# One Trainium2 core, attention and two MoE layers: attention tiles of two heads of both batches, h in matmuls over 64 rows, and phase A in program order

## The chip, the cores and the metric

The kernel runs on one core of a Trainium2 chip. The metric is the device time of one execution in microseconds (us). Times below are in us unless they say ns. The engines are TensorE (PE; its weight loads are listed apart as PEld), VectorE (DVE), ScalarE (ACT), GpSimd (POOL) and SyncE (SP), which issues all DMAs of this kernel.

## What is computed

An attention with 32 memory slots per head, then two layers on its rows (8 batches of 8 heads, 576 positions, head size 64):

```python
a = phi - np.max(phi, axis=2, keepdims=True); a = np.exp(a)
a = a / (np.sum(a, axis=2, keepdims=True) + 1e-09)
k_m = np.einsum('bhsm,bhsd->bhmd', a, k)
v_m = np.einsum('bhsm,bhsd->bhmd', a, v)
scores = (1 / 8) * np.matmul(q, k_m.transpose(0, 1, 3, 2))   # then a softmax over the 32
x = np.matmul(attn, v_m)                                     # as 4608 rows of 512
h = np.maximum(np.maximum(x @ w1, x @ w2), x @ w3)           # 768 wide
x = h @ w_out
...
gate = 1.0 / (1.0 + np.exp(-(x @ w_gate)))                   # 1536 wide
out = (gate * (x @ w_val)) @ w_out2
```

q, k, v and phi are 32-bit; the weights arrive as 64-bit floats.

## The kernel before

**Numbers.** Each operand of a large matmul is split into a high and a low part (type fp32r), and each product is three matmuls (`PASSES`: low by high, high by low, high by high). The 64-bit weights are turned to 32 bits in `w_f32`: two ACT and three DVE instructions on a tile of 128x384 (tiles `raw`, `ca`, `cr`, lines 122 to 126).

**Phase A** computes the attention and the first layer for four pairs of batches (p = 0 to 3) and writes the result x2 to memory. Phase B, from line 667 on, is the second layer; it begins when phase A ends, and the change leaves its code alone.

**Attention tiles.** One tile n holds four heads of one batch: 4 x 32 memory slots are its 128 rows, so a pair of batches has four tiles. A tile runs through stages a0 to a5 (lines 174 to 274): softmax of phi over its positions, a transpose, k_m and v_m in `kvb` (line 206, matmuls that write 32 columns of the array each, four side by side), their transposes (`kt` and the split `vt`), the scores (line 243, 64 columns each, two side by side), and the softmax over 32 slots, which ends in `stg`; `a_split` makes the split tile `attn` (128 x 576) of it.

**G.** x itself is never formed. Since x = attn v_m, x @ w = attn (v_m @ w): `g_step` (line 334 on) makes G = v_m @ w for two heads and for a block j of 128 of the 768 columns of the three weights (384 columns). One result of 128 rows holds 64 rows of one batch and 64 of the other; they go to two tiles, so that each is copied out and split in two halves of 64 rows: two ACT copies (line 354) and two subtractions (line 73), on DVE, or for the first head pair in p = 0 on POOL.

**h.** `h_step(p, j, u)` makes h for a block j and a quarter u of the pair's rows: u is a batch b and a half of its 576 positions (288). For each of the three weights 6 matmuls over all 128 rows (two groups of four heads, three passes) fill one PSUM bank; ACT copies the first, DVE takes the maximum with the second and third, and the result is split into `h`.

**x2.** `x2_step` multiplies h by the first w_out: 18 matmuls for each of 4 blocks of 128 columns and 4 quarters.

**Order.** A pair has 40 steps s: 24 for h (6 blocks j by 4 quarters, with G for block j + 1 beside them in the first 20) and 16 for x2 (with G for the next pair's block 0 in the last four). The attention stages of the next pair, the weights' conversions (`w_step` for the first layer, `b_step` for the 48 tiles of phase B, in pairs 1 to 3 by the program) and the loads are laid beside the steps by position. The program order is only a wish: except for the first loads, the tile framework's scheduler may move each instruction on each engine, by its own timeline. PSUM has 8 banks of 128 x 512, shared by all of phase A (`bank`).

In the parts below, "h stretch" and "x2 stretch" are the parts of a pair from its first matmul of line 367 and of line 390 on.

Of the kernel before, what the change touches and what calls it, by code (L numbers as in the profile page):

```python
# [18 lines left out]
def attn_moe_kernel(  # L19
# [11 lines left out]
    nc = tc.nc  # L31
# [16 lines left out]
    vec, act, pool, pe, sync = nc.vector, nc.scalar, nc.gpsimd, nc.tensor, nc.sync  # L48

    queue = {"in order": True, "last weights": None}  # L50
# [6 lines left out]

    def later(fn, *a):

        with tc.issue_after(queue["last weights"].ins):  # L60
            fn(*a)
# [43 lines left out]
    def w_fetch(pl, src):  # L105
        if not is64:
            w = pl.tile([128, PC], F32, tag="wf", name="wf", bufs=3)
            queue["last weights"] = dma(w, src)
            return w
        raw = pl.tile([128, PC], I64, tag="raw", name="raw", bufs=3)  # L110
        queue["last weights"] = dma(raw, src)
        return raw
# [24 lines left out]
    def early(shape):  # L137

        t = low.tile([128, 2 * U], F32R, tag="h", name="early", bufs=4 * J)
        return f32(t[:, :shape[1]])  # L140

    def load_phi(n):
        st = A[n] = {"kv": [], "q": []}
        if n in (2, 3):
            st["phi"] = early([128, S])
        else:
            st["phi"] = att.tile([128, S], F32, tag="phi", name="phi", bufs=2)
        dma(st["phi"], phiT[n])

    def load_kv(n):  # L150
        for c in range(5):
            if n < 4:
                t = early([128, 512])
            else:
                t = att.tile([128, 512], F32, tag="kv", name="kv", bufs=7)
            if c < 4:
                dma(t, kvm[n, c])
            else:
                dma(t[:64], kvt[n])
            A[n]["kv"].append(t)  # L160

    def load_q(n, e):
        if (n, e) in ((0, 0), (0, 1)):
            t = early([128, S])
        else:
            t = att.tile([128, S], F32, tag="q", name="q", bufs=3)
        dma(t, qT[n, e])
# [6 lines left out]
    def a0(n):  # L174
        st = A[n]
        nm = att.tile([128, 1], F32, tag="nm", name="nm", bufs=4)
        vec.tensor_reduce(out=nm, in_=st["phi"], axis=AX.X, op=ALU.max, negate=True)
        ss = att.tile([128, 1], F32, tag="ss", name="ss", bufs=4)
        et = st["et"] = att.tile([128, S], F32, tag="et", name="et", bufs=2)
        act.activation(out=et, in_=st["phi"], func=AF.Exp, bias=nm, accum_out=ss)  # L180
        rs = st["rs"] = att.tile([128, 1], F32, tag="rs", name="rs", bufs=4)
        vec.tensor_scalar(out=rs, in0=ss, scalar1=EPS, scalar2=None, op0=ALU.add)
        vec.reciprocal(out=rs, in_=rs)
        rm = st["rm"] = att.tile([128, 2], F32, tag="rm", name="rm", bufs=4)
        vec.tensor_scalar(out=rm, in0=mask, scalar1=rs, scalar2=None, op0=ALU.mult)
        yield

    def a1(n):
        st = A[n]
# [4 lines left out]
        yield  # L194
        es = st["es"] = att.tile([128, 5, 128], F32, tag="es", name="es", bufs=2)
# [3 lines left out]
    def a2(n):  # L199
# [20 lines left out]
    def a3(n):  # L220
        st = A[n]
        b, g = divmod(n, 2)
        p = bank()
# [5 lines left out]
        if b % 2 == 0:  # L229
            VT[b // 2, g] = mid.tile([128, 2, 4, 64], F32R, tag="vt", name="vt", bufs=4)  # L230
        vt = VT[b // 2, g]
        src = p[:, 128:256].rearrange("p (h m) -> p h m", h=2)
        for h in range(2):
            x = 3 * h if b % 2 == 0 else 2 - h
            act.copy(vt[:, 0, x], src[:, h])
            sub(vec, vt[:, 1, x], src[:, h], f32(vt[:, 0, x]))

    def a4(n):
# [10 lines left out]
        yield  # L249
        s_t = st["s"] = att.tile([128, S // 32, 32], F32, tag="s", name="s", bufs=2)  # L250
# [6 lines left out]
        mx = att.tile([128, S // 32], F32, tag="mx", name="mx", bufs=2)  # L257
        vec.tensor_reduce(out=mx, in_=s_t, axis=AX.X, op=ALU.max)
        bc = [128, S // 32, 32]
        sub(pool, s_t, s_t, mx.unsqueeze(2).to_broadcast(bc))  # L260
        act.activation(out=s_t, in_=s_t, func=AF.Exp, scale=SC)

    def a5(n):
        st = A[n]
        s_t = st["s"]
        bc = [128, S // 32, 32]
# [4 lines left out]
        pool.tensor_tensor(out=s_t, in0=s_t, in1=sm.unsqueeze(2).to_broadcast(bc), op=ALU.mult)  # L271
        stg = st["stg"] = att.tile([128, S], F32, tag="stg", name="stg", bufs=4)
        vec.transpose(out=stg, in_=s_t.rearrange("p a m -> p (a m)"))
        yield
# [10 lines left out]
    stages = [a0, a1, a2, a3, a4, a5]  # L285
# [13 lines left out]
    def w_have():  # L299
        j, hp, p, w = wq.pop(0)  # L300
        if j < 0:
            w = w_f32(mid, w)
            r = slice(hp * PC, hp * PC + PC)
            w_split(w, wo1_t[:, 0, r], wo1_t[:, 1, r])
            return
        if p == 0:
            w = w_f32(mid, w)
            t = mid.tile([128, 2, PC], F32R, tag="wx", name="wx", bufs=6)
            w_split(w, t[:, 0], t[:, 1])
            dma(wxs[j, hp], f32(t))  # L310
            w = t
        WX[j, hp] = w
# [9 lines left out]
    def b_step():  # L322
        if not bq:
            return
        b_want()
        i, n, w = bq.pop(0)
        dma(wbf[i, :, n * PC:n * PC + PC], w_f32(mid, w))
# [4 lines left out]
    def g_step(p, j, hp):  # L332
        g, e = divmod(hp, 2)
        if e == 0:
            for b in range(2):
                G[b, j, g] = mid.tile([128, 2, 384], F32R, tag=f"g{b}", name=f"g{b}", bufs=3 + b)
        ps = bank()
        vt, w = VT[p, g], WX.pop((j, hp))
        for n, (x, y) in enumerate(PASSES):
            pe.matmul(  # L340
                ps[:, :384],
                lhsT=vt[:, x, 2 * e:2 * e + 2].rearrange("p a m -> p (a m)"),
# [4 lines left out]
        src, eng = ps, vec  # L347
        if p == 0 and hp == 0:
# [518 lines left out]
```

## Time and profile before

| | |
|---|---|
| time, median of 3 runs | 1394.29 (1390.80 to 1395.04) |
| the profiled execution's own time | 1393.47 |
| its span, from first to last instruction | 1391.6 |
| ACT busy | 567.8 (41%), 1204 instructions |
| POOL busy | 519.3 (37%), 454 instructions |
| 1728 matmuls of h (line 367) | 254.6 busy |
| 1152 matmuls of x2 (line 390) | 158.4 busy |
| 288 matmuls of G (line 340) | 71.9 busy |
| mean granted PE clock | 0.986 |

Busy time counts the stretches in which an engine has an instruction under way; matmuls overlap, so that the mean length of one (301 ns for h) is longer than the distance from one to the next. A row of the chain of waits says when a piece of work on the chain that ended last began, how long it took, and which engine, tile and line it was. In a group of instructions the columns are line, engine, operation, tiles, shape, count, then busy time and the mean length of one in ns, then the idle time ahead of them and who ended it.

### The profile page before, as it was taken

What the parts mean: (1) busy time and instruction counts of PE and PEld (TensorE: products, weight loads), DVE (VectorE), ACT (ScalarE), POOL (GpSimd) and SP (SyncE); (2) the same over time, 40 slices, a digit from 0 to 9 for tenths busy, and PEclk for the clock granted to TensorE, in tenths of its full rate; (3) what the DMA queues carried; (4) which work ended last, traced back from release to release, by engine and by line L of the source; (5) the groups of instructions that cost most, each with busy time, mean ns of one, the idle gap of its engine ahead of it and who ended that gap; (6) DMA issues with size and microseconds to landing.
All of it is one profiled execution on the core that took longest, in us unless ns stands there. A gap on an engine that the chain in (4) does not pass through costs nothing.

```text
span 1391.6 us, 22154 instructions
## 1 busy us (share of the span) xinstructions
PE 1335.2 (96%) x7864; PEld 1184.2 (85%) x7864; DVE 872.3 (63%) x1549; ACT 567.8 (41%) x1204; POOL 519.3 (37%) x454
## 2 busy tenths in 40 slices
PE   5688998999999999999999999999999999999998
PEld 3587887889999999788888888888888899999997
DVE  5999989988773575667755345454454544554454
ACT  5787556755653452453343321232222322143221
POOL 2776512241342127554486111371112711161111
PEclk9799999999999999999999999999999999999999
DMA  9589799879644424865557554465455666566661
GB/s 309 192 285 300 258 305 311 287 262 305 212 133 139 129 82 137 295 258 211 202 190 228 175 176 159 155 207 190 158 178 169 217 221 221 195 229 231 221 207 66
DMA packets 112269, 292.43 MB, mean 210 GB/s; under 512 B 12576, under 2 KB 28960, under 8 KB 112160
## 3 DMA queue, kind: packets, MB, share of 16 engines
q1 hardware_dynamic: 112160, 291.03, 62.4%
q8 instruction: 62, 1.02, 0.3%
q14 instruction: 47, 0.39, 0.1%
HBM read 224.92 MB, written 66.06 MB: 209 GB/s over the span
## 4 chain that ended last, share of the span: by engine, by line
PE 80%; DVE 9%; DMA 5%; issue 3%; ACT 1%; POOL 1%; SPq 0%; DVEq 0%; ACTq 0%
PE po L752 21%; PE px L685 16%; PE ps L367 11%; PE pz L685 11%; PE pv L685 10%; PE ps L390 6%; PE ps L340 2%; DVE ca L126 2%; DVE g L73 1%; DVE ca L124 1%; DMA raw<-wb_dram 1%; DVE ca L125 1%; PE ps L206 1%; PE ps L243 1%; DVE hm L378 1%
## 5 line engine op out<-in xcount | busy, mean ns | idle before, releaser
L752 PE MATMUL po<-wo,gg 128*128 128x512 f32 x1296 | 327.7, 392 | 1.0 <-POOL gg L73 1.0
L73 POOL TENSOR_TENSOR gg<-gf,gg 128x512 fp32r<-128x512 f32 (+1 forms) x120 | 143.6, 1197 | 471.1 <-ACT gg L718 430.2
L752 PEld LDWEIGHTS po<-wo,gg 128*128 128x128 f32 x1296 | 242.4, 188 | 49.5 <-POOL gg L73 1.3
L367 PE MATMUL ps<-attn,g 128*128 128x288 f32 x1728 | 254.6, 301 | 19.4 <-DVE g L73 12.4
L367 PEld LDWEIGHTS ps<-attn,g 128*128 128x128 f32 x1728 | 244.2, 193 | 26.9 <-issue 14.0
L685 PE MATMUL px<-xa,tb 128*128 128x512 f32 (+1 forms) x1080 | 244.0, 368 | 3.2 <-DVE x L70 3.2
L764 DVE TENSOR_TENSOR acc<-po,acc 128x512 f32<-128x512 f32 x180 | 124.3, 690 | 176.4 <-PE po L752 176.3
L685 PEld LDWEIGHTS px<-xa,tb 128*128 128x128 f32 x1080 | 198.1, 188 | 31.5 <-DVE x L70 3.6
L685 PE MATMUL pv<-xa,tb 128*128 128x512 f32 (+1 forms) x720 | 169.2, 367 | 0.0
L685 PE MATMUL pz<-xa,tb 128*128 128x512 f32 (+1 forms) x720 | 169.1, 367 | 0.0
L390 PE MATMUL ps<-h,wo 128*128 128x288 f32 x1152 | 158.4, 296 | 0.6 <-DVE hm L379 0.6
L390 PEld LDWEIGHTS ps<-h,wo 128*128 128x128 f32 x1152 | 154.8, 189 | 2.7 <-DVE ca L126 0.9
L73 POOL TENSOR_TENSOR h<-hm,h 128x288 fp32r<-128x288 f32 x96 | 84.1, 880 | 194.0 <-ACT h L68 98.0
L685 PEld LDWEIGHTS pz<-xa,tb 128*128 128x128 f32 x720 | 132.1, 188 | 18.6
L685 PEld LDWEIGHTS pv<-xa,tb 128*128 128x128 f32 x720 | 131.9, 188 | 17.7
L718 ACT CAST gg<-gf 128x512 fp32r<-128x512 f32 (+1 forms) x120 | 69.4, 578 | 178.2 <-DVE gf L714 131.6
L736 DVE TENSOR_TENSOR u<-pz,p 128x512 f32<-128x512 f32 (+1 forms) x120 | 76.2, 635 | 97.8 <-PE pz L685 92.9
L73 DVE TENSOR_TENSOR g<-ps,g 64x384 fp32r<-64x384 f32 x180 | 99.2, 552 | 27.9 <-ACT g L354 24.9
L708 ACT ACTIVATE sg<-sg 128x512 f32<-128x512 f32 (+1 forms) x90 | 53.1, 590 | 144.3 <-DVE sg L706 144.1
L354 ACT CAST g<-ps 64x384 fp32r<-64x384 f32 x192 | 90.4, 472 | 50.8 <-PE ps L340 26.9
L73 POOL TENSOR_TENSOR xa<-xf,xa 128x512 fp32r<-128x512 f32 (+1 forms) x64 | 78.7, 1251 | 18.9 <-ACT xa L131 18.8
L714 DVE TENSOR_TENSOR gf<-gf,sg 128x512 f32<-128x512 f32 (+1 forms) x90 | 71.5, 795 | 9.5 <-ACT sg L708 1.3
(92 smaller groups left out, 1401.5 us busy)
## 6 DMA issues: line engine op xcount, KB each, us to landing
tb<-tbs SPq DMA_DIRECT2D x168, 512.0 KB, 3.8
wx<-wxs SPq DMA_DIRECT2D x72, 384.0 KB, 4.4
wo<-wos SPq DMA_DIRECT2D x48, 512.0 KB, 5.0
tbs<-tb SPq DMA_DIRECT2D x42, 512.0 KB, 2.9
raw<-wb_dram SPq DMA_DIRECT2D x48, 384.0 KB, 5.3
kv<-kvm_dram SPq DMA_DIRECT2D x48, 256.0 KB, 5.2
raw<-wx_dram SPq DMA_DIRECT2D x24, 384.0 KB, 4.3
wxs<-wx SPq DMA_DIRECT2D x24, 384.0 KB, 4.7
```

The costliest lines, as they stand in the source:

```text
L73: eng.tensor_tensor(out=o, in0=a, in1=b, op=ALU.subtract)
L126: vec.scalar_tensor_tensor(out=ai, in0=hi, scalar=0x80000000, in1=ai, op0=ALU.bitwise_and, op1=ALU.bitwise_or)
L354: act.copy(t[r, 0], ps[r, :384])
L367: pe.matmul(ps[w][:, :U], lhsT=G[b, j, g][:, x, 128 * w:128 * w + 128], rhs=at[:, y, hf * U:hf * U + U], start=(n == 0), stop=(n == 5),)
L390: pe.matmul(ps[:, :U], lhsT=wo1_t[:, x, (d * J + j) * 128:(d * J + j) * 128 + 128], rhs=H[u, j][:, y], start=(n == 0), stop=(n == 3 * J - 1),)
L685: pe.matmul(ps[:, :half], lhsT=w[:, a, o:o + 128], rhs=x[:, k, c, :half], start=(first and n == 0), stop=(n == 5), skip_group_check=not first,
L708: act.activation(out=sg, in_=src, func=AF.Sigmoid)
L714: vec.tensor_tensor(out=gf, in0=gf, in1=sg, op=ALU.mult)
L718: act.copy(t[:, 0, :half], gf)
L736: vec.tensor_tensor(out=u, in0=ps[:, :half], in1=E["p1", v], op=ALU.add)
L752: pe.matmul(ps, lhsT=GG[sc, j, c, h][:, x, 128 * m:128 * m + 128], rhs=WO[sc, j, h][:, y], start=(n == 0), stop=(n == 5),)
L764: vec.tensor_tensor(out=t, in0=ps, in1=t, op=ALU.add)
```

## The change

**Tiles.** An attention tile n now holds two heads of both batches of the pair: rows 0 to 63 are batch 0, rows 64 to 127 batch 1 (`source` gives the place in memory, and each load becomes two, of 64 rows, or of half the columns; k and v come in two chunks at once). Then one result of `g_step` is one tile of G: one ACT copy and one DVE subtraction over 128 rows. `vt` is likewise copied and split whole.

**h.** `h_part` makes h for a block j and a half hf of the positions, for both batches, in two steps of 36 matmuls. Each takes 64 rows of G and of `attn`, and those of the two batches alternate, rows 0 to 63 and then 64 to 127, into two different banks. A block and half needs 4 tiles of attention, 3 weights and 3 passes: 36 pairs. ACT copies the first weight's two banks (`h_copy`), DVE takes the maxima (`h_max`), ACT and POOL split both batches at once (`h_keep`).

**Order.** From the first step on, until x2 of the last pair, every compute instruction and DMA keeps the program's order on its engine. A step issues on PE the attention stages, G, then h or x2; then the copies; the conversion; the maximum with the second weight; what follows (the third weight's maximum, x2's copy, h's split, stores) is put off to the next step. The six attention stages become ten, one per step, each tile eight steps after the last. Four conversions of first-layer weights move from ahead of the first step into it, and phase B's conversions stand where the program has them: 13 in pair 1, 13 in pair 2, 22 in the h stretch of pair 3.

On PE, in the h stretch of pair 2, before the change (L340 is G, L367 h, L243 the scores; the numbers tell tiles of G apart):

```order
L340 MATMUL ps<-wx,vt 128x384 x3
L367 MATMUL ps<-attn,g_4841 128x288 x9
L243 MATMUL ps<-q,kt 64x288 x4
L367 MATMUL ps<-attn,g_4962 128x288 x9
L340 MATMUL ps<-wx,vt 128x384 x3
```

The same place in the change (L61 is the wrapper that all engines now go through; wx,vt is G, attn,g is h, each h matmul over 64 rows):

```order
L61 MATMUL ps<-ident,kvb 128x128 x2
L61 MATMUL ps<-wx,vt 128x384 x3
L61 MATMUL ps<-attn,g 128x288 x36
L61 MATMUL ps<-q,kt 64x288 x4
L61 MATMUL ps<-wx,vt 128x384 x3
L61 MATMUL ps<-attn,g 128x288 x36
```

The attention stage now stands ahead of G and G ahead of h, and h is never interrupted; 18 matmuls of a step have become 36.

On DVE, late in phase A before the change (hm are the maxima for h, g the subtractions for G over 64 rows):

```order
L378 TENSOR_TENSOR hm<-ps,hf 128x288
L379 TENSOR_TENSOR hm<-ps,hm 128x288
L73 TENSOR_TENSOR g_5285<-ps,g_5285 64x384
L70 CAST h<-hm 128x288
L378 TENSOR_TENSOR hm<-ps,hf 128x288
L73 TENSOR_TENSOR g_5284<-ps,g_5284 64x384
L379 TENSOR_TENSOR hm<-ps,hm 128x288
```

And in the h stretch of pair 3 in the change (the three instructions on ca are one conversion):

```order
L61 TENSOR_TENSOR hm<-ps,hm 128x288 x4
L61 TENSOR_TENSOR g<-ps,g 128x384
L61 TENSOR_SCALAR ca<-ca 128x384
L61 ISA ca<-ca,cr 128x768
L61 SCALAR_TENSOR_TENSOR ca<-raw,ca 128x384
L61 TENSOR_TENSOR g<-ps,g 128x384
```

The cast is gone to ACT, two subtractions have become one, and a conversion of phase B's weights stands in each step between the subtraction for G and the maxima.

The diff's core:

```diff
+    class InOrder:
...
+                ins = fn(*a, **k)
+                if order["kept"]:
+                    tc.keep_in_program_order(ins)
+    def source(n, b):
+        p, hp = divmod(n, 4)
+        g, pr = divmod(hp, 2)
+        return 2 * (2 * p + b) + g, pr ^ b
...
     def g_step(p, j, hp):
...
-        for hf in range(2):
-            r = slice(64 * hf, 64 * hf + 64)
-            t = G[(hf + e) % 2, j, g]
-            act.copy(t[r, 0], ps[r, :384])
-            sub(eng, t[r, 1], src[r, :384], f32(t[r, 0]))
+        t = G[j, hp] = mid.tile([128, 2, 384], F32R, tag="g", name="g", bufs=8)
+        act.copy(t[:, 0], ps[:, :384])
+        sub(vec, t[:, 1], ps[:, :384], f32(t[:, 0]))
...
+    def h_part(p, j, hf, first):
+        if first:
+            HP[j, hf] = []
+        for w, hp in [(w, hp) for w in range(3) for hp in range(4)][slice(0, 6) if first else slice(6, 12)]:
+            if hp == 0:
+                HP[j, hf].append([bank() for _ in range(2)])
+            at = AT[4 * p + hp]
+            for n, (x, y) in enumerate(PASSES):
+                for b in range(2):
+                    r = slice(64 * b, 64 * b + 64)
+                    pe.matmul(
+                        HP[j, hf][w][b][:, :U],
+                        lhsT=G[j, hp][r, x, 128 * w:128 * w + 128],
+                        rhs=at[r, y, hf * U:hf * U + U],
+                        start=(hp == 0 and n == 0), stop=(hp == 3 and n == 2),
+                    )
+    def h_max(j, hf, w):
+        m = HM[j, hf]
+        for b in range(2):
+            vec.tensor_tensor(out=m[:, b], in0=HP[j, hf][w][b][:, :U], in1=m[:, b], op=ALU.max)
+    def h_keep(j, hf):
+        m = HM.pop((j, hf))
...
+        act.copy(t[:, 0], m)
+        sub(pool, t[:, 1], m, f32(t[:, 0]))
...
-        t = low.tile([128, U], F32, tag="x2", name="x2", bufs=3)
+        t = low.tile([128, U], F32, tag="x2", name="x2", bufs=2)
...
+    order["kept"] = queue["in order"] = True
...
         for s in range(NS + NX):
             if last and s == NS:
+                order["kept"] = queue["in order"] = False
...
+            take("first")
+            gens = [stages[k](n) for k, n in sorted(atts.get(s, ()), reverse=True)]
+            for x in gens:
+                next(x)
+            g = None
             if s < NS:
                 j, u = divmod(s, 4)
                 if j + 1 < J:
+                    g = g_step(p, j + 1, u)
+                    next(g)
+                h_part(p, j, u // 2, u % 2 == 0)
...
+            if s < NS and u % 2:
+                h_copy(j, u // 2)
+            take("splits")
+            if g:
+                next(g, 1)
+            for x in gens:
+                next(x, 1)
+            take("hold")
             for fn, a in side.get(s, ()):
                 fn(*a)
+            for fn, a in convs.get(s, ()):
+                fn(*a)
+            if s < NS and u % 2:
+                h_max(j, u // 2, 1)
+                later["first"].append(lambda j=j, hf=u // 2: h_max(j, hf, 2))
+                hold.append(lambda j=j, hf=u // 2: h_keep(j, hf))
...
+            take("stores")
```

More of the change, by code (lines that the diff above doesn't have):

```diff
@@ L107, in w_fetch @@
             w = pl.tile([128, PC], F32, tag="wf", name="wf", bufs=3)
[L108 removed]
+            dma(w, src)
             return w
         raw = pl.tile([128, PC], I64, tag="raw", name="raw", bufs=3)
[L111 removed]
+        dma(raw, src)
         return raw
@@ L135, in attn_moe_kernel, with early_tile, early @@
     A = {}
-    def early(shape):
-        t = low.tile([128, 2 * U], F32R, tag="h", name="early", bufs=4 * J)
-        return f32(t[:, :shape[1]])
+    halves = []
+    def early_tile():
+        return f32(low.tile([128, 4 * U], F32R, tag="h", name="early", bufs=2 * J))
+    def early(cols):
+        if not halves:
+            t = early_tile()
+            halves.extend((t[:, :2 * U], t[:, 2 * U:]))
+        return halves.pop(0)[:, :cols]
+    def source(n, b):
+        p, hp = divmod(n, 4)
+        g, pr = divmod(hp, 2)
+        return 2 * (2 * p + b) + g, pr ^ b
     def load_phi(n):
@@ L228, in a3, with a5 @@
         act.copy(kt, p[:, 0:128])
[L229 to L238, printed above, removed]
+        vt = VT[n] = mid.tile([128, 2, 128], F32R, tag="vt", name="vt", bufs=8)
+        act.copy(vt[:, 0], p[:, 128:256])
+    def a5(n):
         st = A[n]
@@ L332, in g_step @@
     def g_step(p, j, hp):
[L333 to L336, printed above, removed]
         ps = bank()
-        vt, w = VT[p, g], WX.pop((j, hp))
+        vt, w = VT[4 * p + hp], WX.pop((j, hp))
         for n, (x, y) in enumerate(PASSES):
@@ L574, in attn_moe_kernel, with take, at @@
         run(g_step(0, 0, hp))
-    for hp in range(4):
-        w_step()
     bplan = [(j + h * NJ, n) for j in range(NJ) for h in range(2) for n in range(4)]
-    def b_start():
-        while len(bq) < 2 and bplan:
-            b_want()
+    order["kept"] = queue["in order"] = True
+    due = {"first": [], "splits": [], "hold": [], "stores": []}
+    def take(what):
+        fns, due[what] = due[what], []
+        for fn in fns:
+            fn()
     for p in range(NP):
         last = p == NP - 1
-        side = {}
-        def at(pos, fn, *a):
-            side.setdefault(min(int(pos), NS + NX - 1), []).append((fn, a))
+        side, loads, convs = {}, {}, {}
+        def at(pos, fn, *a, where=None):
+            where = side if where is None else where
+            where.setdefault(min(int(pos), NS + NX - 1), []).append((fn, a))
         if last:
```

272 lines of the change are left out of this document (152 added, 120 removed).

## The prediction

> **What bounds the kernel now.** I read first the page's span and its busy rows in 40 slices, to see where TensorE is not the bound.
>
> ```profile
> span 1391.6 us, 22154 instructions
> PE   5688998999999999999999999999999999999998
> DVE  5999989988773575667755345454454544554454
> ```
>
> TensorE (PE) is full from about slice 9 on; before that, VectorE (DVE) is as full as PE. Phase A, which the change touches, is the first 16 slices. So I cut it at the first matmul of each h stretch (line 367) and of each x2 stretch (line 390) of the four pairs of batches, and asked for the busy time of each engine in each piece. Columns: stretch, its length, then PE, weight load, DVE, ACT, POOL busy with instruction counts, granted PE clock, DMA share, GB/s.
>
> ```profile
> 0.00:50.80 50.80, 26.91 (x235) 14.83 (x235) 34.89 (x78) 29.22 (x73) 22.20 (x24) 0.88 0.91 291
> 50.80:150.30 99.50, 86.56 (x605) 79.17 (x605) 97.57 (x186) 75.52 (x178) 66.53 (x61) 0.92 0.77 259
> 150.30:203.70 53.40, 49.48 (x409) 45.89 (x410) 45.58 (x98) 29.51 (x71) 16.54 (x14) 0.97 0.90 294
> 203.70:294.00 90.30, 83.75 (x660) 76.74 (x658) 86.43 (x189) 61.18 (x148) 29.33 (x29) 0.96 0.86 291
> 294.00:339.60 45.60, 44.39 (x357) 42.73 (x356) 36.92 (x81) 24.40 (x57) 10.08 (x8) 1.00 0.90 297
> 339.60:418.50 78.90, 78.90 (x661) 74.61 (x660) 60.03 (x135) 46.58 (x114) 27.18 (x30) 1.00 0.56 175
> 418.50:462.40 43.90, 43.90 (x355) 42.54 (x354) 13.43 (x28) 11.09 (x26) 8.14 (x8) 1.00 0.41 136
> 462.40:529.70 67.30, 67.30 (x490) 67.30 (x490) 45.33 (x93) 34.46 (x82) 18.56 (x23) 1.00 0.31 93
> 529.70:572.50 42.80, 39.64 (x296) 39.02 (x294) 26.30 (x30) 13.28 (x24) 32.57 (x22) 1.00 0.67 229
> ```
>
> Pairs 0 to 3 have an h stretch and an x2 stretch each. Pair 2 does the same matmuls as pair 1, and takes 78.9 + 43.9 = 122.8 where pair 1 takes 90.3 + 45.6 = 135.9 and pair 0 99.5 + 53.4 = 152.9. In pairs 0 and 1 DVE is busy 97.57 of 99.5 and 86.43 of 90.3: **there it is DVE that ends last, in pairs 2 and 3 it is PE.** Pair 3 has no attention beside it: 67.3 is the bare length of 432 h matmuls and 60 for G, and 78.9 - 67.3 = 11.6 is what three tiles of attention add in pair 2, 3.9 each. The prize of relieving DVE is at most 152.9 + 135.9 - 2 x 122.8 = 43 of 1391.6.
>
> What fills DVE is in the same stretches for the conversions alone (three DVE instructions each; columns DVE, ACT, POOL):
>
> ```profile
> 50.80:150.30 99.50, 50.49 (x69) 23.81 (x45) 24.51 (x22) 0.92 0.77 259
> 203.70:294.00 90.30, 35.68 (x60) 10.89 (x20) 0.00 (x0) 0.96 0.86 291
> 339.60:418.50 78.90, 2.94 (x6) 1.11 (x2) 0.00 (x0) 1.00 0.56 175
> ```
>
> A conversion costs DVE 50.49 / 23 = 2.2 in pair 0 (with POOL busy) and 35.68 / 20 = 1.78 in pair 1. All 48 of phase B's are over early in pair 2: the scheduler pulls them forward.
>
> **The change, part by part.**
>
> *G's copies and the casts.* In DVE's groups from 50 to 150:
>
> ```profile
> L73 DVE TENSOR_TENSOR g<-ps,g 64x384 fp32r<-64x384 f32 x33 | 18.1, 550 | 0.6
> L70 DVE CAST h<-hm 128x288 fp32r<-128x288 f32 x6 | 3.2, 533 | 0.0
> ```
>
> Two subtractions over 64 rows become one over 128, taken at the same 0.55, since each row still has 384 elements. Pair 0 gave 12 of its 48 halves to POOL, so DVE goes from 36 to 24: 12 x 0.55 = 6.6 less; the casts go to ACT: 3.2 less; by the end of pair 0's h stretch 28 conversions are needed where 30 had been made: 4.4 less. That is 14, so DVE alone could end the stretch near 136. In pairs 1 to 3, 24, 24 and 20 subtractions go (13, 13, 11 us).
>
> *Pair 0's start.* A step now takes all four tiles of attention at once (line 409), so the first needs the fourth tile; now that one comes while the third step waits:
>
> ```profile
> 64.94 0.76 DVE L273 STREAM_TRANSPOSE stg<-s 128x576 f32<-128x576 f32 x1
> 66.47 1.81 PE L367 MATMUL ps<-attn,g 128*128 128x288 f32 x6 [1.20 <-ACT attn L281]
> ```
>
> In the new order DVE has one conversion, four half subtractions' worth, four maxima and a cast less ahead of that transpose, 2.2 + 2.2 + 1.8 + 1.1 = 7.3, so it comes near 58 and the first step passes its ninth pair near 60. From there PE's own length is 67.3, less 1.2 for the half step done, plus 2.2 tiles of attention, 8.5, plus the mode changes below, 6.8: end near 141.5. PE and DVE are then nearly equal; I allow 4 for their waiting on each other: 145.5, not 150.3. The x2 stretch becomes PE's: 43.9 with one tile of attention in it, and 1.75 tiles here, so 46.8. Pair 0 ends at 192 where it ended at 203.7: **-11.5.**
>
> *Pairs 1 and 2.* 13 conversions each, one in three steps: DVE falls in pair 1 to 86.4 - 35.7 - 13 - 3 + 8 x 1.78 = 49. Pair 1 comes to pair 2's length: **-13**; pair 2 gains nothing.
>
> *The h matmuls.* 1728 matmuls over 128 rows become 1728 pairs over 64 rows. Whether a pair goes side by side is not in the trace for rows; for columns it is (chain of waits, start, length, what):
>
> ```profile
> 418.17 0.44 PE ps L192 x4
> 418.60 0.11 PE ps L193
> 418.71 4.79 PE ps L390 x36
> 423.50 1.36 PE ps L206 x40
> 424.87 2.58 PE ps L390 x18
> 427.44 0.22 PE ps L225 x2
> 427.66 2.37 PE ps L390 x18
> ```
>
> A matmul over the full array with 128 moving columns takes 0.11 (line 192); line 206, four side by side in 32 columns each, takes 1.36 / 40 = 0.034, so four in 0.136. Taken so for rows, a pair costs what one full matmul did, 2.37 / 18 = 0.132; **I add 0.001 for the second's issue: +1.7.** From below, 0.12 (some of the 0.132 hidden by the other half): -20; from above, two loads and two matmuls in turn, under the rivals.
>
> The Trainium skill, page "TensorE: Matmul & The Clock Gate", section Part 3 on packing small matmuls, says that matmuls in different row groups of the array run at the same time, starting about 4 ns apart. By it, as an estimate, a pair costs 0.004 more than one matmul, 1728 x 0.004 = 6.9, and the sum below would be 5 higher; the 0.034 of line 206 shows the same for columns, and no run here shows it for rows yet.
>
> *Mode changes.* After line 206 the next 18 matmuls take 2.58, not 2.37: 0.21 to come back to the full array. The way in, and a change from 128 to 64 rows that stands inside line 206's own block, cost 1.36 - 10 x 0.11 = 0.26 for two, 0.13 each. The 64-row form loads 128 columns of weights as the full one does, so I take 0.18, nearer the dearer row; ends 0 and 0.21. G's matmuls are over 128 rows, h's over 64, and they alternate in 20 of 24 steps: two changes a step. Less the changes that attention makes already, that is some 40 more per pair: 7.2. In pairs 1 to 3, where PE is the bound: **+21.6.** Nothing hides them there.
>
> The Trainium skill, page "TensorEngine Tiling (Array Packing)", section Tiling Modes, says that changing the mode, not just the tile, drains the engine. By it each alternation pays, as the 0.21 and 0.13 above do; without it the sum below would be 21.6 lower.
>
> *Pair 3's conversions.* 22 of them now stand in its h stretch, in order. DVE: 45.3 - 11 - 1.9 + 22 x 1.78 = 71.6, against PE's 67.3 + 7.2 = 74.5. PE covers it by 3; were the mode changes free, DVE would set 71.6, 4 over today.
>
> *Waits added by the order.* On DVE the maximum that frees a bank stands behind the step's conversion, which waits for ACT and its DMA, and PE waits for that bank; on SP each store stands behind the loads of its step; the first x2 step waits for the last h's POOL split, now of 576 elements. In pairs 1 to 3 DVE's step (subtraction 0.55, maxima 0.9, conversion 1.78: 3.2) is shorter than PE's (2.38 + 0.53 + 0.36 = 3.3), and 8 banks hold two steps: **+4** in all; ends 0 and +28. The DMAs are more and smaller (phi in two, k and v in 1 KB pieces), behind a DMA share of 0.3 to 0.9; I count nothing while they are asked for a tile ahead. Phase B, from 572.5, keeps its code: nothing.
>
> **Sum**, against the profiled execution's own 1393.5 (span 1391.6): -11.5 - 13 + 1.7 + 21.6 + 4 = +2.8, so **1396**. The median shown, 1394.3, is 0.8 above that execution, inside its spread.
>
> **The rivals.**
> *Free changes of mode.* If rows switch without drain, pairs 1 to 3 lose 21.6 less, pair 0 some 6 less, and pair 3 pays 4 for DVE: 1396 - 21.6 - 6 + 4 = 1372. For it: only 0.13 of the rows above is a change of rows. Against: that one is not nothing, and it stood in the same block.
> *Slower: the conversion in DVE's queue.* If a step of DVE with conversion, subtraction, maxima and an attention transpose pair (1.78 + 0.55 + 0.9 + about 1.7 = 4.9) overtakes PE's 3.6, PE waits for a bank. That decides from 3.6 on. Of 48 conversions in pairs 1 to 3, about half meet such a neighbour or a late load; at 1.0 each +24: 1420. For it: 97.57 of 99.5 in pair 0 today, and order that no longer bends. Against: means of 2 to 3 per step there.
> *The change does not go side by side.* Weight loads by width, in the groups by form:
>
> ```profile
> L367 PEld LDWEIGHTS ps<-attn,g 128*128 128x128 f32 x1728 | 244.2, 193 | 26.9 <-issue 14.0 <-DVE hm L379 4.7 <-DVE hm L378 4.5
> L206 PEld LDWEIGHTS ps<-kv,es 128*32 128x32 f32 x384 | 9.7, 109 | 2.0 <-issue 1.0 <-DVE hm L378 0.3 <-ACT cr L123 0.3
> ```
>
> 96 columns more cost 0.084, so 128 cost 0.112. If the two loads of a pair go in turn, a pair takes 0.224, not 0.132: 1728 x 0.092 = +159, 1555. Against: the 0.034 of line 206, whose loads must overlap too.
>
> **How the numbers follow.** Forecast, 1386 to 1406: 0.44. Free changes, 1364 to 1384: 0.22. DVE's queue, 1407 to 1432: 0.24. Not side by side, over 1500: 0.10. About 0.3% (4 us) is what a measurement of this kernel can tell from no change. Faster than 1390: a fifth of the forecast and all of the second, 0.09 + 0.22, 0.31. Within: 0.45 of the forecast, 0.20. Slower: the rest of the forecast, 0.15, and the last two, 0.49. The range, 1365 to 1430, leaves out the last rival and the rims of the two beside the forecast.
>
> **What would show it.** Pairs 0 to 3 should take, to their next start, about 142, 132, 132 and 118, where now 153, 136, 123 and 110. The h rows should come in pairs, 18 of them in 2.4; 2.58 or more would be the drain. In pair 3 DVE should be near 71 busy. I am wrong in kind if 18 pairs take 4, if pair 2 gets no longer, or if PE's idle time before h is put down to the maxima.

## The result, and the profile after

The change made the kernel slower: 1428.45 us (median of 4 runs, 1427.97 to 1429.5) against 1392.55 before (4 runs, 1388.18 to 1395.04), a ratio of 1.026 (95% interval 1.023 to 1.029). The forecast was 1396; the range, up to 1430, held the time by 1.5.

From the page of the changed kernel, the span and the same two rows of 40 slices as in the prediction:

```profile
span 1426.6 us, 25129 instructions
PE   5598999999999999799999999999999999999998
DVE  4777736755766686666775445554355544454454
```

In slices 2 to 9 DVE is not as full as it was (8 and 9 before, 3 to 7 now); in slices 13 to 16, where phase B's conversions now stand, it is fuller (3 to 7 before, 6 to 8 now). PE has a gap in slice 17. So the relief of DVE came in pairs 0 and 1, and yet phase A is longer. The stretches by the same cuts as before (columns: stretch, length, then PE, weight load, DVE, ACT, POOL busy with counts, granted clock, DMA share, GB/s; h and x2 stretches of pairs 0 to 3 from the second row on):

```profile
0.00:49.20 49.20, 30.35 (x235) 16.57 (x235) 29.68 (x64) 24.11 (x57) 15.43 (x18) 0.89 0.89 266
49.20:160.10 110.90, 92.34 (x1078) 78.54 (x1077) 85.03 (x175) 61.77 (x142) 50.20 (x42) 0.88 0.65 213
160.10:210.60 50.50, 47.87 (x372) 45.23 (x368) 23.32 (x48) 17.99 (x42) 16.92 (x14) 0.97 0.68 204
210.60:297.40 86.80, 86.25 (x1087) 73.71 (x1086) 57.84 (x124) 39.28 (x95) 20.45 (x16) 1.00 0.62 200
297.40:342.70 45.30, 44.86 (x360) 43.02 (x358) 25.08 (x48) 15.83 (x36) 11.79 (x9) 1.00 0.75 251
342.70:429.50 86.80, 86.25 (x1087) 73.70 (x1086) 57.74 (x124) 39.29 (x95) 20.46 (x16) 1.00 0.63 192
429.50:474.70 45.20, 44.94 (x362) 43.05 (x360) 24.72 (x48) 16.37 (x36) 12.05 (x10) 1.00 0.68 226
474.70:555.50 80.80, 78.34 (x922) 68.19 (x921) 64.43 (x127) 42.05 (x98) 15.65 (x12) 1.00 0.76 235
555.50:607.00 51.50, 41.64 (x296) 40.61 (x296) 29.39 (x36) 14.13 (x27) 34.27 (x23) 0.91 0.66 219
```

| | before | forecast | after |
|---|---|---|---|
| end of pair 0 | 203.7 | 192 | 210.6 |
| pair 1 | 135.9 | 132 | 132.1 |
| pair 2 | 122.8 | 132 | 132.0 |
| pair 3, to the matmul of phase B that ends the wait | 110.1 | 118 | 129.4 |
| from there to the end | 819.1 | 819.1 | 822.5 |

Pairs 1 and 2 are as forecast to 0.1. What was missed is 18.6 in pair 0, 11.4 in pair 3 and 3.4 at the start of phase B.

PE's timeline shows the two prices of the new matmuls. First a step of pair 3 before the change, then one of pair 2 after it; in both only G and h follow each other (start, length, engine, line, tiles, shape, count; lengths overlap, so read the distance between starts):

```profile
470.62 0.69 PE L340 MATMUL ps<-wx,vt 128*128 128x384 f32 x3
471.15 2.56 PE L367 MATMUL ps<-attn,g 128*128 128x288 f32 x18
473.54 0.69 PE L340 MATMUL ps<-wx,vt 128*128 128x384 f32 x3
```

```profile
345.76 0.34 PE L61 MATMUL ps<-wx,vt 128*128 128x384 f32 x1
346.03 2.63 PE L61 MATMUL ps<-attn,g 64*128 64x288 f32 x36
348.59 0.79 PE L61 MATMUL ps<-wx,vt 128*128 128x384 f32 x3
349.31 2.66 PE L61 MATMUL ps<-attn,g 64*128 64x288 f32 x36
```

36 matmuls over 64 rows take 348.59 - 346.03 = 2.56, where 18 over 128 rows took 2.39 here and 2.37 in the prediction's chain: they do go side by side, and 0.17 to 0.19 is added. G takes 349.31 - 348.59 = 0.72 instead of 471.15 - 470.62 = 0.53: 0.19 more. A step is 3.28 where it was 2.92: two mode changes of 0.18 to 0.19, forecast 0.18.

The chain of waits in pair 3's h stretch (start, length, who) is the picture of the miss:

```profile
508.09 0.49 ACT g L61
508.64 0.57 DVE ca L61
509.26 0.44 issue
509.71 0.46 DVE hm L61
510.21 5.12 PE ps L61 x51
```

The same five lines come again from 515.36 on, once in two steps: PE stands until a maximum (`hm`) frees a bank, and that maximum follows a conversion (`ca`). DVE's timeline at the place shows why (idle time ahead and its cause in brackets):

```profile
503.95 0.55 DVE L61 TENSOR_TENSOR g<-ps,g 128x384 fp32r<-128x384 f32 x1
505.23 1.25 DVE L61 TENSOR_SCALAR ca<-ca 128x384 uint32<-128x384 uint32 x1 [0.73 <-ACT ca L61]
506.61 0.56 DVE L61 CUSTOM_DVE_ANT_0 ca<-ca,cr 128x768 uint16<-128x768 uint16 x1
507.21 0.56 DVE L61 SCALAR_TENSOR_TENSOR ca<-raw,ca 128x384 uint32<-128x384 uint32 x1
507.68 0.55 DVE L61 TENSOR_TENSOR g<-ps,g 128x384 fp32r<-128x384 f32 x1
508.15 0.35 DVE L61 TENSOR_SCALAR ca<-ca 128x384 uint32<-128x384 uint32 x1
508.64 0.56 DVE L61 CUSTOM_DVE_ANT_0 ca<-ca,cr 128x768 uint16<-128x768 uint16 x1
509.23 0.56 DVE L61 SCALAR_TENSOR_TENSOR ca<-raw,ca 128x384 uint32<-128x384 uint32 x1
509.71 1.54 DVE L61 TENSOR_TENSOR hm<-ps,hm 128x288 f32<-128x288 f32 x4
```

Between two groups of maxima stand two steps' conversions and subtractions, and the first conversion makes all of them wait for ACT. DVE is busy only 64.43 of the 80.80: it isn't full, but its maxima come late for PE. At the end of phase A the chain reads:

```profile
595.33 0.47 SPq L70
595.89 3.17 DMA x2s<-x
599.37 4.02 DMA x2s<-x
603.51 0.47 DVE x L61
604.12 4.75 PE px L61 x12
```

The same place before the change:

```profile
561.90 3.99 DMA x2s<-x
567.98 3.93 DMA x2s<-x
572.54 1.66 PE px L685 x6
```

After PE's last x2 matmul (594.2) two stores of x2 now stand in series before the last copy out of PSUM may run. Before the change one did; the store at 561.90 ran while PE still made x2 (until 567.7), and PE did six matmuls of phase B (from 567.8) ahead of the wait. PE, now idle for 9.66, does its first 12 matmuls of phase B in 4.75 where the next group of 12 takes 2.72: from 604.1 to 608.85 the granted clock was 0.60, and 1.00 in the stretch after it. Before the change it was 1.00 throughout this place.

### The profile page after: what moved, and what is told of

It reads as the page before. It is cut to its first block, busy times and chain, and to the rows that moved or that the text cites. A ratio compares the mean times of both kernels' runs of the same rounds, so it can differ in the third digit from the quotient of the medians.

```text
span 1426.6 us, 25129 instructions
## 1 busy us (share of the span) xinstructions
PE 1367.4 (96%) x9592; PEld 1184.2 (83%) x9592; DVE 818.6 (57%) x1425; ACT 514.2 (36%) x1062; POOL 485.4 (34%) x394
## 4 chain that ended last, share of the span: by engine, by line
PE 81%; DVE 8%; DMA 4%; issue 2%; ACT 2%; POOL 2%; SPq 0%; DVEq 0%; ACTq 0%; POOLq 0%
PE ps L61 24%; PE po L61 21%; PE px L61 16%; PE pz L61 10%; PE pv L61 10%; DVE ca L61 4%; DMA early<-kvm_dram 1%; DVE hm L61 1%; DMA raw<-wx_dram 1%; DVE sm L61 1%; ACT g L61 1%; POOL xf L61 1%; DVE g L61 1%; DMA x2s<-x 1%; ACT ca L61 0%
## 5 line engine op out<-in xcount | busy, mean ns | idle before, releaser
L61 PE MATMUL po<-wo,gg 128*128 128x512 f32 x1296 | 327.8, 392 | 1.0 <-POOL gg L61 1.0
L61 POOL TENSOR_TENSOR gg<-gf,gg 128x512 fp32r<-128x512 f32 (+1 forms) x120 | 143.1, 1192 | 474.2 <-ACT gg L61 433.2
L61 PE MATMUL ps<-attn,g 64*128 64x288 f32 x3456 | 263.8, 300 | 21.1 <-DVE hm L61 9.6
L61 PEld LDWEIGHTS po<-wo,gg 128*128 128x128 f32 x1296 | 242.4, 188 | 49.5 <-POOL gg L61 1.3
L61 PEld LDWEIGHTS ps<-attn,g 64*128 64x128 f32 x3456 | 237.9, 186 | 49.0 <-issue 20.3
L61 PE MATMUL px<-xa,tb 128*128 128x512 f32 (+1 forms) x1080 | 245.7, 370 | 9.7 <-DVE x L61 9.7
L61 PEld LDWEIGHTS px<-xa,tb 128*128 128x128 f32 x1080 | 199.5, 189 | 38.2 <-issue 9.9
L61 DVE TENSOR_TENSOR acc<-po,acc 128x512 f32<-128x512 f32 x180 | 124.3, 690 | 175.9 <-PE po L61 174.9
L61 PE MATMUL pv<-xa,tb 128*128 128x512 f32 (+1 forms) x720 | 169.5, 367 | 0.0
L61 PE MATMUL pz<-xa,tb 128*128 128x512 f32 (+1 forms) x720 | 169.1, 367 | 0.0
L61 PE MATMUL ps<-h,wo 128*128 128x288 f32 x1152 | 159.9, 297 | 0.2 <-ACT h L61 0.2
L61 PEld LDWEIGHTS ps<-h,wo 128*128 128x128 f32 x1152 | 155.7, 189 | 2.9 <-issue 1.5
L61 PEld LDWEIGHTS pz<-xa,tb 128*128 128x128 f32 x720 | 132.1, 188 | 18.6
L61 PEld LDWEIGHTS pv<-xa,tb 128*128 128x128 f32 x720 | 131.9, 188 | 17.7
L61 ACT CAST gg<-gf 128x512 fp32r<-128x512 f32 (+1 forms) x120 | 69.4, 578 | 177.9 <-DVE gf L61 173.5
L61 DVE TENSOR_TENSOR u<-pz,p 128x512 f32<-128x512 f32 (+1 forms) x120 | 76.2, 635 | 94.9 <-PE pz L61 90.4
L61 POOL TENSOR_TENSOR h<-hm,h 128x576 fp32r<-128x576 f32 x48 | 68.7, 1432 | 174.1 <-ACT h L61 173.6
L61 ACT ACTIVATE sg<-sg 128x512 f32<-128x512 f32 (+1 forms) x90 | 53.1, 590 | 142.7 <-DVE sg L61 142.6
L61 DVE TENSOR_TENSOR g<-ps,g 128x384 fp32r<-128x384 f32 x96 | 53.1, 553 | 78.7 <-ACT g L61 78.6
L61 POOL TENSOR_TENSOR xa<-xf,xa 128x512 fp32r<-128x512 f32 (+1 forms) x64 | 79.2, 1259 | 22.2 <-ACT xa L61 18.8
L61 DVE TENSOR_TENSOR hm<-ps,hm 128x288 f32<-128x288 f32 x192 | 75.1, 449 | 10.5 <-PE ps L61 10.4
L61 ACT CAST g<-ps 128x384 fp32r<-128x384 f32 x96 | 46.2, 481 | 89.0 <-PE ps L61 88.5
```

What stands on the lines that cost most here:

```text
L61: ins = fn(*a, **k)
```

## The experiments

Two theories of the miss. **Order:** the kept order puts waits on the path, above all the conversion ahead of the maximum in DVE's queue; the tiles themselves cost what was forecast. **Form:** the new tiles, their matmuls and smaller DMAs cost more than forecast. All medians are against the kernel before on the same chip (1391.5 to 1393.0).

**1. Without the kept order.** The new tiles, with the scheduler free as before the change.

```diff
-    order["kept"] = queue["in order"] = True
+    order["kept"] = queue["in order"] = False
```

> The change's tiles, but the scheduler may move instructions in phase A again. Theory: the 64-row matmuls cost some 0.19 per change of mode (40 changes, 7.5 per pair, in pairs 1 to 3), and the kept order costs the rest, in pair 0 (h stretch 110.9 where PE alone needs some 82), in pair 3's h stretch (80.8, PE's own length 75) and ahead of phase B. Then pairs 1 and 2 stay near 132, pair 0's h stretch falls to 90 to 100, pair 3's to 75, and the time is 1395 to 1412. Rival, the order costs everything: 1393 or less. Rival, the tiles cost everything: 1425 or more.

The edit frees the compute instructions and the DMAs alike. Measured 1490.56, ratio 1.071 (1.069 to 1.073): a miss. The h stretches of pairs 2 and 3 came as expected, 85.5 and 74.8 instead of 86.8 and 80.9, but those of pairs 0 and 1 took 162.8 and 108.8. The heading of the chain of waits from 40 to 260 names what stands there:

```profile
by line: DMA raw<-wb_dram 23.6%; issue 10.0%; DVE ca L61 9.3%; DMA phi<-phiT_dram 4.2%; ACT ca L61 4.1%; DMA raw<-wo_dram 3.2%; DMA x2s<-x 2.1%; ACT cr L61 2.1%; DVE hm L61 1.6%; POOL wx L61 1.4%; ACT et L61 1.0%; POOL h L61 0.9%; ACT h L61
```

The free scheduler pulls phase B's loads (`wb_dram`, from 151.8 to 305.6) and conversions into pairs 0 and 1. It did so before the change too (from 150.6 to 335.9); why it costs so much more with the new tiles was not tried. For this program the kept order is worth 62, though it costs some 6 in pair 3. So the order as a whole isn't the fault; what in it costs pair 0 and pair 3 their time is asked below.

**2. The split for x2 behind G's copy and the attention stages.**

```diff
-            take("splits")
             if g:
                 next(g, 1)
             for x in gens:
                 next(x, 1)
+            take("splits")
```

> ACT's split of the converted weights moves behind G's copy and the attention's ACT work in each step. Theory: in pair 0 a loop runs through the queues once a step, conversion on DVE (2.0), split on ACT (0.5), G's copy on ACT (0.5), subtraction for G on DVE (0.55), next conversion; it makes the 4.4 of a step. With the split behind G's copy the loop loses 0.5 and a wait of about 0.4 per step: the h stretch of pair 0 goes from 110.9 to 95 to 100, the time to 1414 to 1418. Rival, pair 0 waits for its DMAs on SP's ordered queue (48 of waiting for conversions there): the stretch stays within 3 of 110.9, the time within 3 of 1428.

Measured 1419.62, 1.020 (1.019 to 1.022). Pair 0's h stretch went from 110.8 only to 109.4, not to 95 to 100: the theory missed, and the split isn't what holds that stretch. But pair 0's x2 stretch fell from 50.6 to 46.4 (the prediction's 46.8). The rest is 1.3 ahead of the first h matmul (47.9 instead of 49.2), 1.3 from pair 3's x2 stretch on, and small pieces.

**3. Three x2 buffers again** (paid for with one `vt`).

```diff
-        vt = VT[n] = mid.tile([128, 2, 128], F32R, tag="vt", name="vt", bufs=8)
+        vt = VT[n] = mid.tile([128, 2, 128], F32R, tag="vt", name="vt", bufs=7)
...
-        t = low.tile([128, U], F32, tag="x2", name="x2", bufs=2)
+        t = low.tile([128, U], F32, tag="x2", name="x2", bufs=3)
```

> A third buffer for x2's copies, as before the change (its room comes from two unused ones of vt's eight: seven are kept). Theory: after the last x2 matmul the last two copies each wait for a store to land (3.2 and 4.0 in the chain), and phase B's first matmuls wait for them; from the last x2 matmul to the end it is 832.4 with the change and 823.9 before. With three buffers one store's wait goes: 826 to 829, the time 1422 to 1425. Rival, the wait is for the copies of x and of the weights' sums on POOL: no change from 832, 1428.

Measured 1422.94, 1.022 (1.020 to 1.024), as expected. From the last x2 matmul to the end takes 828.6 instead of 832.4, and after that matmul only one store is left in the chain ahead of phase B. So of the 8.5 that this piece had grown (from 823.9), 3.8 went with the second store. The buffer is one way to lose it, and not the only one: number 5, with two buffers and this part of the program as in the change, also has one store there, and takes 829.2. Of the other 4.7, the slow first matmuls are over 2 (12 take 5.36 here, at a granted clock of 0.52); the rest wasn't tried.

**4. G for two steps in one go**, which halves the alternations.

```diff
-                if j + 1 < J:
+                if j + 1 < J and u % 2 == 0:
                     g = g_step(p, j + 1, u)
                     next(g)
+                    g2 = g_step(p, j + 1, u + 1)
+                    next(g2)
```

> G is made for two steps at once, so that 72 matmuls of h stand between, not 36. Nothing else moves. Theory: each change between the full array and 64 rows costs about 0.19; 10 round trips fewer per pair are 20 x 0.19 = 3.8 less in each of pairs 1 to 3, 11 in all: 1417, with the h stretch of pairs 1 and 2 at 83 instead of 86.8. Rival, PE's extra length is waiting for banks and copies: the stretches stay within 1 of 86.8, the time within 3 of 1428.

Measured 1412.74, 1.015 (1.013 to 1.017), below the 1417 expected. The h stretches of pairs 1 and 2 fell from 86.8 to 82.8, as expected: 10 alternations fewer of two changes each, 4.0 / 20 = 0.20 a change. Pair 3's fell by 5.7, more than the changes explain.

**5. The three passes of one batch, then those of the other**, instead of alternating.

```diff
-            for n, (x, y) in enumerate(PASSES):
-                for b in range(2):
+            for b in range(2):
+                for n, (x, y) in enumerate(PASSES):
```

> The same 64-row matmuls, but for each head pair and weight the three passes of one batch come first and then the three of the other, so that neighbours mostly use the same rows. Theory, matmuls over different rows run side by side and each costs 0.133 alone: six matmuls take four slots instead of three (only the last of one batch and the first of the other overlap), so a step grows by 6 x 0.133 = 0.8, 19 per pair in pairs 1 to 3 and up to that in pair 0: 1485 to 1505. Rival, pairs are not side by side but run in turn at half the length: no change from 1428.

Measured 1425.17 in one run: no loss, where the theory had 1485 to 1505. The rival's number came, but its reason (matmuls in turn at half the length) is ruled out by number 9. PE's timeline at the place shown above:

```profile
346.04 2.63 PE L61 MATMUL ps<-attn,g 64*128 64x288 f32 x36
348.60 0.79 PE L61 MATMUL ps<-wx,vt 128*128 128x384 f32 x3
```

Again 2.56. Started strictly in program order, two of three matmuls of a row group would have to wait for the one before them; six would take four times 0.132, and 36 about 3.2 (an estimate). The Trainium skill, page "TensorE: Matmul & The Clock Gate", section Part 3 on packing small matmuls, says that matmuls start and end in program order; with number 9, this run speaks against it for two row groups. The trace does not name the batch of a matmul, so that the matmuls reached PE in the order of the program is taken from the kernel and not seen.

**6. No conversions in pair 3**, all of them in pairs 1 and 2.

```diff
-            n_b = 22 if last else 13
+            n_b = 0 if last else 24
```

> The 22 conversions of pair 3's h stretch go to pairs 1 and 2, 24 each over their 40 steps. Theory: in pair 3 PE waits for the second weight's maximum, which stands behind a conversion on DVE, and later for a conversion that waits for its store; without conversions that stretch takes PE's own 75, as in the run without kept order (74.8), not 80.9, and pairs 1 and 2, where DVE is busy 83 of 132, take the 11 more each with at most 3 of loss: 1420 to 1425. Rival, the same wait just moves into pairs 1 and 2: they grow by 3 or more each and the time stays within 3 of 1428.

Measured 1434.02, 1.030 (1.027 to 1.032): a miss, by the rival. Pair 3's h stretch is 74.8, as expected, so the 6 there are the conversions. But pairs 1 and 2 each got 7.5 longer (h 91.6, x2 48.0). The window of pair 1's h stretch in this kernel:

```profile
209.80:301.40 91.60, 88.74 (x1088) 75.68 (x1087) 69.84 (x142) 45.02 (x109) 20.68 (x16) 0.98 0.70 224
```

DVE is busy 69.84 of 91.60. 13 conversions in a pair's 40 steps are all but free (PE is busy 86.25 of 86.80), 24 cost 7.5, long before DVE is full.

**7. Edits 2, 4 and 6 together.**

> The paired G, the late split and the early conversions together. If the three are separate prices (mode changes 15.7, the split's place 8.8, pair 3's conversions 5), they add up: 1428 - 29 = 1397 to 1402. If the paired G's surplus over the 11 expected came from pair 3's waits, the sum is some 5 short: 1402 to 1407.

Measured 1420.4, 1.020 (1.018 to 1.023): a miss, above both ranges. Pair 3's h stretch fell to 70.4, all of it PE's, but the conversions in pairs 1 and 2 ate the gain (h 84.9 and 88.4, x2 48.6 and 48.5).

**8. Four buffers for raw weights, and one more ahead.** Is it SP or the loads that hold pair 0?

```diff
-        raw = pl.tile([128, PC], I64, tag="raw", name="raw", bufs=3)
+        raw = pl.tile([128, PC], I64, tag="raw", name="raw", bufs=4)
...
-        vt = VT[n] = mid.tile([128, 2, 128], F32R, tag="vt", name="vt", bufs=8)
+        vt = VT[n] = mid.tile([128, 2, 128], F32R, tag="vt", name="vt", bufs=6)
...
-        stg = st["stg"] = att.tile([128, S], F32, tag="stg", name="stg", bufs=4)
+        stg = st["stg"] = att.tile([128, S], F32, tag="stg", name="stg", bufs=3)
...
-        while plan and len(wq) < 2:
+        while plan and len(wq) < 3:
```

> Four buffers, not three, for the weights as they arrive, and three fetches ahead instead of two, in pair 0 (room from unused buffers of vt and stg). Theory A: pair 0's steps are slow because SP, in order, waits for the buffer of a conversion three back and then issues the next fetch and the attention's loads late (SP waits for conversions 48 in that stretch); then pair 0's h stretch falls from 110.8 to 100 or less, the time to 1418 or less. Theory B: they are slow since ACT and DVE hand each other the conversion, G's copy and the subtraction in turn within each step, both in order; then it falls by at most 3, 1425 to 1429.

Measured 1444.03, 1.037 (1.035 to 1.039): outside both ranges. Pair 0's h stretch stayed (112.0). The h stretches of pairs 1 to 3 got longer (94.5, 89.6, 86.1). Up to 600, SP waits 135.1 for PE's matmuls, 9.2 at the longest, where it waits 105.0 and 4.8 in the changed kernel. So it seems, and is not shown by itself, that a load asked for a step earlier now waits on SP for a weight buffer that matmuls still read, and all else on SP waits behind it. The edit changed several things; it speaks against a lack of raw buffers in pair 0 and says nothing else.

**9. Both batches over the same rows** (batch 1's h is computed from batch 0's rows).

```diff
-                    r = slice(64 * b, 64 * b + 64)
+                    r = slice(0, 64)
```

> The h matmuls of both batches take rows 0 to 63 (batch 1's h is computed from batch 0's rows; everything else, G, copies, conversions, DMAs and the order, stays). Theory (the change's pairs go side by side because they stand in different rows): with the same rows the two of a pair go in turn, each step of 18 pairs takes 18 x 0.132 = 2.4 more, 24 steps 57 more per pair of batches: pairs 1 to 3 have h stretches of about 140 to 145 instead of 86.8, 86.8 and 80.9, pair 0 about 150, and the whole 1428 + 3 x 57 + 40 = about 1640. Rival (the pair costs one matmul for another reason, such as half the rows): the pitch stays 133 ns a pair and the whole 1425 to 1432.

Measured 1676.48 in one run. PE's timeline:

```profile
346.21 5.00 PE L61 MATMUL ps<-attn,g 64*128 64x288 f32 x36
351.15 0.79 PE L61 MATMUL ps<-wx,vt 128*128 128x384 f32 x3
```

4.94 for 36 instead of 2.56. The h stretches of pairs 1 and 2 grew by 55.9 (57 expected), pair 0's by 87.0, more than expected. It is the different rows that make a pair cost one matmul.

**10. Pair 0 without DVE's share of the conversions** (these three instructions are left out in pair 0's steps; what is converted there are the first layer's weights, so those come out wrong, and not phase B's as the expectation has it; loads, stores, ACT's and POOL's work and the order remain).

```diff
+        if order["skip"]:
+            return a
...
+            order["skip"] = p == 0
             split, store = w_have()
+            order["skip"] = False
```

> Leaves out the DVE instructions of the weight conversions in pair 0's steps (phase B's weights are then wrong); loads, stores, ACT's and POOL's work, the order and all waits that remain stay. Theory (DVE's share of a conversion, kept in order between the maxima, is what pair 0 pays): the h stretch of pair 0 falls from 110.8 to 85 to 92, near pair 1's 86.8, and the whole by 19 to 26, to 1403 to 1410. Rival (the wait for loads and stores on SP, or ACT's and POOL's share, paces the steps): it stays above 103, the whole above 1420.

Measured 1409.62 in one run, 18.8 less. The h stretch of pair 0 fell to 98.2: not as far as the 85 to 92 expected, and below the 103 above which the rival had it. The window of that stretch and of the part from its second step on, and below them the same 23 steps of the changed kernel:

```profile
47.80:146.00 98.20, 86.63 (x1078) 74.62 (x1077) 51.80 (x117) 60.76 (x142) 50.62 (x43) 0.91 0.74 241
65.60:146.00 80.40, 80.40 (x1039) 70.00 (x1038) 41.54 (x98) 53.83 (x128) 39.41 (x34) 1.00 0.75 244
67.60:160.10 92.50, 85.36 (x1039) 73.29 (x1038) 73.42 (x153) 54.82 (x128) 38.76 (x33) 0.96 0.64 209
```

From its second step on PE is busy 80.40 of 80.40, with all the DMAs of the change beside it. The expectation had forgotten the first step, whose last 16 matmuls wait until 62.1 for the fourth attention tile, so that the second begins at 65.6. In the changed kernel the same 23 steps take 160.0 - 67.6 = 92.4: the conversions cost 12.0 there, 2.0 ahead of it, and 4.4 in the x2 stretch (50.6 to 46.2). Pair 0 ends at 192.2 instead of 210.6. The last two rows show that the 12.0 is not all idle time: PE stands for 7.1, and is busy 5.0 longer with the same matmuls, at a granted clock of 0.96 against 1.00.

**11. The good edits together:** 2 and 3, and G for two steps in pair 0 and for all four steps of a block j in pairs 1 to 3.

```diff
+                k = 4 if p else 2
+                if j + 1 < J and u % k == 0:
+                    gs = [g_step(p, j + 1, u + i) for i in range(k)]
...
```

> Three edits that were each faster or neutral alone, on different places: the split for the next x2 stretch behind the G copy and the attention stages (-9 alone), three x2 buffers and seven vt (-5.5 alone), and the G matmuls of two steps (pair 0) or of all four steps of an h tile (pairs 1 to 3) in one go. If mode changes cost 0.19 each wherever they stand, pairs 1 to 3 go from 20 alternations to 5 (two changes each): 15 x 2 x 0.18 = 5.4 less each, h stretches of 81.4, 81.4 and 75; the whole 1428 - 9 - 4 - 16 - 3 = 1396, 1392 to 1401, level with the kernel before. Rival (four G tiles at once hold PE's banks, and the copies behind them make the maxima late): pairs 1 to 3 stay at 83 or more, the whole 1404 to 1412.

Measured 1405.36, 1.009 (1.008 to 1.011): a miss. The time lies in the rival's range, though the rival's condition did not come: the h stretches of pairs 1 to 3 are 80.2, 80.2 and 74.8, in pairs 1 and 2 6.6 less for 30 changes fewer, 0.22 each. But pair 0 kept 105.2; its h begins later, at 53.8, and it ends at 207.2, only 3.4 earlier. The x2 stretches of pairs 1 and 2 grew by 1.4 to 46.7, for which no cause was sought. The chain of this kernel in pair 0:

```profile
100.00 1.58 DVE ca L61
101.60 0.57 DVE ca L61
102.61 0.57 ACT ca L61
103.20 0.87 DVE ca L61
104.20 0.57 DVE ca L61
104.79 0.56 DVE ca L61
105.34 0.43 DVE hm L61 x2
```

Two whole conversions, with a wait for ACT between them, stand ahead of the maxima.

**12. Number 11 with the maximum ahead of the conversion.**

```diff
+            if s < NS and u % 2:
+                h_max(j, u // 2, 1)
             for fn, a in convs.get(s, ()):
                 fn(*a)
             if s < NS and u % 2:
-                h_max(j, u // 2, 1)
```

> e11 (1405.4 against 1392.8) with one more edit: in each step the maximum with the second weight stands ahead of the conversion on DVE, not behind it. Theory (the place of the conversion in DVE's queue is the price: PE waits for banks that the maximum frees, and the maximum waits for ACT's and DVE's halves of a conversion): pair 0's h stretch falls from 105.2 toward the 98.2 that it has with no DVE conversion at all, to 98 to 101, pair 3's from 74.8 to 70 to 72, and the whole to 1394 to 1399. Rival (it is the amount of DVE work in a kept order, wherever it stands; the maximum waits for PE and now holds the conversion back, which comes late for its store and the next load): pair 0 stays at 103 to 109, pair 3 above 74, the whole 1403 to 1412.

Measured 1399.37 (6 runs), 1.006 (1.0045 to 1.0077). Pair 0's h stretch fell to 100.1, as the theory had it, with DVE busy 83.35 in it (85.64 in number 11); pair 3's only to 73.8, not to 70 to 72, and the whole is just above the theory's upper edge. The place of the conversion is thus shown to be a price by itself, but not the whole price. Pair 0 ends at 201.1 instead of 207.2, and without DVE's conversions it ended at 192.2: 6 of 15 (that 100.1 looks so near number 10's 98.2 comes of h beginning at 53.1 and not at 47.8). In pair 3 the place gave 1.0, where number 6 found 6.1 for the conversions as a whole. What the rest is, the amount of DVE's work or another wait in the kept queues, was not tried. It is the best version found, and still slower than the kernel before.

## Why the prediction was wrong where it was

The forecast's 1396 was 32 too low. That the range held the time was luck as far as the forecast's mechanism goes: its upper end was drawn round the slower rival. Two of its terms fell, one edit had no term, and the other terms stood.

- **"I add 0.001 for the second's issue: +1.7"** stood: 2.56 for 18 pairs, of which 0.17 to 0.19 is the mode change, leaves the 2.37 to 2.39 of the old 18. Number 9 shows that the rows do it. The 4 ns a pair of the Trainium skill (page "TensorE: Matmul & The Clock Gate", section Part 3 on packing small matmuls) would have made 2.44, by the prediction's estimate.
- **"In pairs 1 to 3 ... +21.6"** stood in pairs 1 and 2: 0.18 to 0.19 a change in the trace, 0.20 and 0.22 by numbers 4 and 11, forecast 0.18. The rival of free changes is out. The Trainium skill, page "TensorEngine Tiling (Array Packing)", section Key Properties, says that a change of mode drains the engine; the runs agree, with that price.
- **"Pair 1 comes to pair 2's length: -13"** stood, with DVE at 57.8 (forecast 49): pair 1 takes 132.1, pair 2 132.0.
- **Pair 0, "-11.5", failed: +6.9.** The failed step is "PE and DVE are then nearly equal; I allow 4 for their waiting on each other". With DVE's conversions out of the way (number 10) pair 0 ends at 192.2, and the 18.4 between that and 210.6 is these conversions in DVE's kept queue. That 192.2 is the forecast's 192 is in part luck: the rest of the first step comes at 62.1 there and not "near 60", and PE alone needs 83.9 from then on where the forecast had 81.5; the allowance of 4 about covers both. The step took DVE's work as a sum that packs. Before the change it did pack, 97.57 busy of 99.50; there the scheduler could let a maximum pass a conversion, and the trace has one so (L378 at 99.77, between two instructions on `ca` at 98.85 and 100.13). That this freedom is what let it pack is argued, not shown. In the kept order DVE is busy 85.03 of 110.90, and PE waits 6.1 for maxima, of the 7.1 that it stands in the 23 steps. Of the other 5.0 in the 12.0 the granted clock explains about 80.40 / 0.96 - 80.40 = 3.4, an estimate from the rows of number 10.
- **"Waits added by the order ... +4; ends 0 and +28" was mis-sized.** By its own end of +28 it could have held most of this. In pair 3 the conversions cost 6.1 (80.9 against 74.8 in number 6): "PE covers it by 3" compared totals, DVE 71.6 against PE 74.5, and DVE was even lighter, 64.4. The totals do not say when PE gets its banks. Where in the queue the maximum stands is worth 1.0 by number 12; the rest stays open.
- **One edit had no term: x2's buffers, three to two.** A third buffer took 3.8 off (number 3), about one store (4.02) in the chain ahead of phase B; the same store also went, with two buffers, in number 5. After the pause the first matmuls ran slowly: 4.75 for 12 against 2.72, at a granted clock of 0.60. "Phase B keeps its code: nothing" overlooked that its start waits for phase A's last copies.

By the prediction's own last sign it was wrong in kind: of PE's idle time before h, 9.6 is put down to the maxima, where it was 5.3 before the change; the other 11.4 are the attention tiles of pair 0's first step. This is the group of h's matmuls in the changed kernel; behind the second bar stand the idle time ahead of them and its causes.

```profile
L61 PE MATMUL ps<-attn,g 64*128 64x288 f32 x3456 | 263.8, 300 | 21.1 <-DVE hm L61 9.6 <-ACT attn L61 8.0 <-POOL attn L61 3.4
```

The **slower rival**, the conversion ahead of the maximum, is the nearest to what happened, and its 1420 (1407 to 1432) is the nearer of the two figures. Its point of decision was right in kind: pairs 1 and 2, with 13 conversions in 40 steps, pay nothing, pair 3 with 22 in 24 pays 6, and number 6 with 24 in 40 pays 7.5 a pair. But it placed none of its price in pair 0, where most of it fell, and argued from "97.57 of 99.5 in pair 0 today" without applying it there. Its chance of 0.24 against the forecast's 0.44 was the wrong way round.

What is left after numbers 11 and 12 is 7.6 in the medians (1399.4 against 1391.8) and 5.8 in the profiled executions. There the last x2 matmul comes at 568.8, and before at 567.7, so phase A has become nearly equal; the other 4.6 follow it (828.5 against 823.9).

## What to carry to other kernels

An engine's total in a stretch bounds what order can reach only if something may reorder it; once the order is fixed, ask for each instruction that frees a buffer what stands ahead of it in its queue, and try it first there; here that gave back 6 of 15 in pair 0. A wait of PE cost more than its own length where the granted clock fell with it. Two matmuls over different halves of the rows cost here what one over all rows did, but a change between the forms cost 0.2 each time, so do many of one form, then many of the other. When a rewrite shrinks a buffer count to make room, price that edit like any other: it shows at the seams, where the next phase waits for the last stores.

## What was not expected of the hardware

PE ran the two row groups side by side although the program has three matmuls of one group in a row (number 5): 2.56 for 36 either way. And matmuls that all take the same 64 rows need (4.94 - 0.19) / 36 = 0.132 each (number 9), as long as one over 128 rows (0.132): half the rows saved nothing by themselves.
